# One tile of a windowed-attention and SwiGLU kernel written in token order, its last rows projected as 384 and 128 columns

## The chip, the cores and the metric

The kernel runs on one core of a Trainium2 chip. The metric is device time in microseconds: the median of repeated runs. A profile of one execution shows where that time goes. Engines are named as the profile names them: PE is the matrix engine (PEld its weight load), DVE the vector engine, ACT the scalar engine, POOL GpSimd, and SP the engine that only issues transfers and waits.

## The reference

The reference is attention in a sliding window, followed by a gated feed-forward block on the joined heads:

```python
# q, k, v: (8, 8, 576, 64)
scores = np.matmul(q, k.transpose(0, 1, 3, 2)) / np.sqrt(64)
mask = (rel >= 0) & (rel < 64)          # rel = query position - key position
attn = softmax of the masked scores
x = np.matmul(attn, v), heads joined: (4608, 512)
g = x @ w_gate                          # 512 -> 1536
out = (g * sigmoid(g)) * (x @ w_val) @ w_out   # -> (4608, 512) float32
```

## The kernel before

The 4608 tokens are nine tiles of 512 (`NT = 9`). Tiles 0 to 6 are the first 512 tokens of batches 0 to 6; tile 7 (`LAST`) gathers the 64 remaining tokens of each of the eight batches; tile 8, the last in order, is the first 512 tokens of batch 7. All engines' programs are written out by hand in the order of the code; nothing is reordered by a planner.

For one tile the work is this. `turn_q` and `turn_k` (DVE) transpose the staged queries and keys, which POOL loaded with `load_qk`. `scores` multiplies keys with queries, ACT takes the exponential, DVE masks it. `sums` multiplies the weights with ones (`totals`, line 294), and ACT turns those sums into inverses by a logarithm (`log`, line 304) and an exponential (`invert`, line 307). `mix_all` multiplies the values with the weights (line 347), and `scale` (line 359) multiplies each of the four results, 128 x 512 in PSUM, with the inverse sums, giving `xT`. `gate_value` then runs 12 blocks of four matmuls for the gate and four for the value (line 401); ACT applies SiLU (394) and DVE multiplies into `hT` (395). `project` multiplies 128 columns of `hT` at a time with `w_out` (12 matmuls, line 410), copies the 128 x 512 result to SBUF (`project_end`, line 417) and stores it.

The 512 tokens of a tile do not stand in order. For tile 0 (`t < TURNED`, `TURNED = 1`) column 128 e + x of `xT` is token 4 x + e, for the others column 32 e + x is token 16 x + e. The 128 rows that come out of one `project` are therefore four runs of 32 rows, and the rows of one run lie 16 rows apart in the output. So a tile other than tile 0 needs four stores of 32 rows each per `project`:

```python
for i in range(4):
    eng = nc.scalar if t == NT - 1 and i % 2 else nc.sync
    eng.dma_start(rows[4 * s + i], os_[32 * i:32 * i + 32])
```

In tile 0 one store takes all 128 rows (line 420). In tile 8, where nothing follows, every second store is issued by ACT in place of SP.

The attention of tile t is interleaved with the projection of tile t-1; the gate blocks of tile t carry the turns of tile t+1. Tile 8's projection stands alone at the end: `project` for the row groups 0, 1 and 2, then `project_last` for group 3. That one works in two halves of 256 columns (24 matmuls, line 446), copies each half as it is done (line 450) and stores it in four pieces (line 453), so eight stores in all.

A transfer from SP or ACT reports its landing on one of eight semaphores. At the end of the program SP waits for these in turn (line 717), and then all engines meet before the program ends.

The functions that the change touches follow, with the line numbers that the profile uses.

Of the kernel before, what the change touches and what calls it, by code (L numbers as in the profile page):

```python
# [8 lines left out]
P = 128  # L9
# [8 lines left out]
def kernel(  # L18
# [10 lines left out]
    nc = tc.nc  # L29
    S, D, H = 576, 64, 8  # L30
    NTOK, DFF, DM = 4608, 1536, 512
    NT = NTOK // 512
    TURNED = 1
# [15 lines left out]
    wo = cst.tile([P, 12, DM], BF16, name="wo")  # L49
# [12 lines left out]
    def batch(t):  # L62
        return t if t < LAST else t - 1
# [7 lines left out]
    staged, queries, weights, inverse, xT, hT = {}, {}, {}, {}, {}, {}  # L71
# [169 lines left out]
    def half(x):  # L241
        return slice(64 * x, 64 * x + 64)
# [48 lines left out]
    def totals(t, w, d):  # L291
        for h in range(2):
            for x in range(2):
                nc.tensor.matmul(  # L294
                    d[x][half(h)].rearrange("r (e j y) -> r j e y", e=16, j=8),
                    ones[half(x), 0:D],
                    weights[t, w, h][1][half(x)].rearrange("r j (e y) -> r j e y", e=16),
                )

    def room(n):  # L300
        return fsb.tile([P, 2, 512], FP32, name="r", tag="r", bufs=4)[:, 0:n]

    def log(r, d_ps):
        nc.scalar.activation(r, d_ps, AF.Ln)  # L304

    def invert(r):
        nc.scalar.activation(r, r, AF.Exp, scale=-1.0)  # L307

    def sums(t, w):
        d = d_tile(), d_tile()  # L310
        totals(t, w, d)
        for x in range(2):
            r = room(1)[:, 0]
            log(r, d[x])
            invert(r)
            inverse[t, 2 * w + x] = r

    def sums_wide(t, w):
        d_ps, r = wide("d_ps"), room(2)
        totals(t, w, (d_ps[:, 0], d_ps[:, 1]))  # L320
        for x in range(2):
            inverse[t, 2 * w + x] = r[:, x]
        log(r, d_ps[:])
        invert(r)
# [31 lines left out]
    def scale(t, u, o_ps):  # L356
        if u == 0:
            xT[t] = att.tile([P, 4, 512], BF16, name="xT", tag="xT")
        nc.vector.tensor_mul(xT[t][:, u, :], o_ps, inverse.pop((t, u)))  # L359

    def values_first(u, o_ps):
        mix_first(u, o_ps)
        scale(0, u, o_ps)

    def wide(name):
        return ps_a.tile([P, 2, 512], FP32, name=name, tag="a")

    def d_tile():
        return ps_f.tile([P, 512], FP32, name="d_ps", tag="v")[:]

    def mix_all(t):
        tiles = wide("ao_ps"), wide("ao_ps")
        for w in range(2):
            mix(t, w, (tiles[w][:, 0], tiles[w][:, 1]))
        for u in range(4):
            scale(t, u, tiles[u // 2][:, u % 2])
# [38 lines left out]
    def project_end(t, s, o_ps, copy=nc.vector.tensor_copy):  # L415
        os_ = fsb.tile([P, 512], FP32, name="os_", tag="os_", bufs=4)
        copy(os_[:], o_ps[:])
        rows = out[S * batch(t):S * batch(t) + 512]
        if t < TURNED:
            nc.sync.dma_start(rows.rearrange("(r e) f -> e r f", e=4)[s], os_[:])  # L420
            return
        if t == LAST:
            rows = out.rearrange("(b s) f -> b s f", s=S)[:, 512:S]
            rows = rows.rearrange("b (r e) f -> e b r f", e=16)
        else:
            rows = rows.rearrange("(r e) f -> e r f", e=16)
        for i in range(4):
            eng = nc.scalar if t == NT - 1 and i % 2 else nc.sync
            eng.dma_start(rows[4 * s + i], os_[32 * i:32 * i + 32])

    def out_tile():
        return ps_f.tile([P, 512], FP32, name="o_ps", tag="g")

    def project(t, s):
        o_ps = out_tile()
        project_part(t, (s,), (o_ps,), range(12))
        project_end(t, s, o_ps)

    def project_last(t, s):
        rows = out[S * batch(t):S * batch(t) + 512].rearrange("(r e) f -> e r f", e=16)  # L440
        os_ = fsb.tile([P, 512], FP32, name="os_", tag="os_", bufs=4)
        tiles = out_tile(), out_tile()
        for x in range(2):
            f = slice(256 * x, 256 * x + 256)
            for c in range(12):
                nc.tensor.matmul(  # L446
                    tiles[x][:, 0:256], hT[t][:, c, P * s:P * s + P], wo[:, c, f],
                    start=(c == 0), stop=(c == 11),
                )
            nc.vector.tensor_copy(os_[:, f], tiles[x][:, 0:256])  # L450
            for i in range(4):
                eng = nc.scalar if i % 2 else nc.sync
                eng.dma_start(rows[4 * s + i][:, f], os_[32 * i:32 * i + 32, f])

    def set_exp():
        nc.scalar.preload_act_table_set("natural_log_exp_and_others")  # L456
# [27 lines left out]
    for a in range(2):  # L484
        tr = tri[64 * a:64 * a + 64]
        nc.gpsimd.affine_select(
            out=tr[:, 1 - a], in_=tr[:, 1 - a], compare_op=ALU.is_ge, fill=0.0,
# [3 lines left out]
            out=tr[:, a], in_=tr[:, a], compare_op=ALU.is_ge, fill=0.0,  # L491
# [78 lines left out]
    d_ps, r = wide("d_ps"), room(2)  # L570
    for u in range(2):
        totals_first(u, d_ps[:, u])
        inverse[0, u] = r[:, u]
    log(r, d_ps[:])
    invert(r)
    scores_first(3)
# [27 lines left out]
    for m in range(12):  # L604
# [15 lines left out]
        if 5 <= m < 9:  # L620
            u = m - 5
            join(on_a, keys[:, u], raw_k[:, 2 * u:2 * u + 2])
        if 6 <= m < 10:
            u = m - 6
# [8 lines left out]
    tiles = [ps_f.tile([P, 512], FP32, name="o_ps", tag=x) for x in "gvgv"]  # L633
# [15 lines left out]
    for s in range(4):  # L649
        project_end(0, s, tiles[s], on_a if s < 2 else on_v)  # L650

    for t in range(1, NT):
        if t > 1:
            set_exp()
            scores(t, 0)
            project(t - 1, 0)
            if t == 2:
                stage_v(3)
            o_ps = out_tile()
            project_part(t - 1, (1,), (o_ps,), range(5))  # L660
            scores(t, 1)
            sums(t, 0)
            project_part(t - 1, (1,), (o_ps,), range(5, 12))
            project_end(t - 1, 1, o_ps)
            project(t - 1, 2)
            sums(t, 1)
            mix_all(t)
            project(t - 1, 3)
# [21 lines left out]
    for s in range(3):  # L690
        project(NT - 1, s)
    project_last(NT - 1, 3)

# [28 lines left out]
```

## Time and profile before

| | |
|---|---|
| median of 3 runs | 328.39 us (328.15 to 329.25) |
| span of the profiled execution, first to last instruction | 326.2 us |
| PE busy | 315.9 us, 97% of the span |
| DVE busy | 220.2 us, 67% |
| ACT busy | 167.2 us, 51% |
| POOL busy | 142.8 us, 44% |
| granted PE clock, mean | 0.999 |

The profile gives no other time for the profiled execution than its span. The median of the runs is 2.2 us longer; that part lies outside of the first and the last recorded instruction. In the profile's rows an instruction group is given by line, engine, operation, what it writes and reads, its shape and count; then the busy time and the mean of one in ns, and the idle time before it with what ended it. In the chain of work that ended last, each piece is the one that released the next. In a timeline, rows marked SPq or ACTq are transfers being issued: the time is that of the issuing, not of the data.

### The profile page before, as it was taken

The numbers are of one execution on the slowest core, as the hardware profiler recorded it, in microseconds if no ns is written. First come the engines' busy times: TensorE is split into PE (matmuls) and PEld (weight loads), VectorE is DVE, ScalarE is ACT, GpSimd is POOL, SyncE is SP. The second block draws the span as 40 slices with busy tenths as digits, with TensorE's granted clock in tenths as the row PEclk, the third lists the DMA queues.
The fourth block names the chain that finished last, engine by engine and source line by source line (L and its number), as shares of the span: only waits on it lengthen the run. The fifth ranks groups of instructions, "written<-read, shape, count | busy, mean of one in ns | idle before, by whom it ended". The sixth has DMA issues, their size and how long they took to land.

```text
span 326.2 us, 6959 instructions
## 1 busy us (share of the span) xinstructions
PE 315.9 (97%) x2700; PEld 150.7 (46%) x2743; DVE 220.2 (67%) x352; ACT 167.2 (51%) x239; POOL 142.8 (44%) x256
## 2 busy tenths in 40 slices
PE   8899999999999999999999999999999999999995
PEld 3444444444444444444444544454444544444443
DVE  5865755587766776887678766876697586773431
ACT  5855557337733683358336743565347633773300
POOL 5944545986085893586024989464200000000000
PEclk9999999999999999999999999999999999999999
DMA  7999999999789999959812999799401300020013
GB/s 253 200 202 202 206 146 215 170 146 143 164 160 206 138 151 205 192 81 214 175 38 29 169 173 92 53 191 195 97 2 34 99 0 2 16 83 32 2 33 98
DMA packets 82865, 40.84 MB, mean 125 GB/s; under 512 B 64272, under 2 KB 78352, under 8 KB 82832
## 3 DMA queue, kind: packets, MB, share of 16 engines
q0 software_dynamic: 50672, 23.08, 57.7%
q1 hardware_dynamic: 31136, 16.26, 19.3%
q10 hardware_dynamic: 1024, 1.05, 1.1%
q8 instruction: 21, 0.34, 0.4%
q14 instruction: 12, 0.10, 0.1%
HBM read 54.00 MB, written 9.44 MB: 194 GB/s over the span
## 4 chain that ended last, share of the span: by engine, by line
PE 86%; DMA 8%; POOL 3%; issue 1%; DVE 1%; SPq 0%; DVEq 0%; POOLq 0%
PE o_ps L410 28%; PE g_ps L401 26%; PE v_ps L401 25%; DMA wv<-in_moe_w_val_dram 4%; DMA q_s<-in_q_dram 3%; PE s_ps L261 3%; PE ao_ps L347 2%; PE d_ps L294 1%; DMA q_f<-in_q_dram 1%; POOL wg L172 1%; POOL wv L172 1%; PE o_ps L446 1%; POOL v L129 1%; POOL qk_b L517 0%; DVE qT L198 0%
## 5 line engine op out<-in xcount | busy, mean ns | idle before, releaser
L394 ACT ACTIVATE sg<-g_ps 128x512 f32<-128x512 f32 x108 | 64.4, 597 | 113.8 <-PE g_ps L401 85.1
L395 DVE TENSOR_TENSOR hT<-sg,v_ps 128x512 bf16<-128x512 f32 x108 | 74.7, 693 | 59.8 <-PE v_ps L401 49.2
L401 PE MATMUL g_ps<-xT,wg 128*128 128x512 bf16 x415 | 108.2, 379 | 0.9
L401 PE MATMUL v_ps<-xT,wv 128*128 128x512 bf16 x415 | 107.2, 379 | 0.1
L410 PE MATMUL o_ps<-wo,hT 128*128 128x512 bf16 x396 | 93.6, 380 | 1.5 <-issue 0.3
L108 POOL DMA_DIRECT2D k_s<-in_k_dram x112 | 60.6, 552 | 26.2 <-DMA q_s<-in_q_dram 15.3
L401 PEld LDWEIGHTS <-wv 128*128 128x128 bf16 x424 | 41.5, 98 | 50.1
L401 PEld LDWEIGHTS <-wg 128*128 128x128 bf16 x424 | 41.3, 98 | 49.5 <-issue 0.6
L410 PEld LDWEIGHTS <-hT 128*128 128x128 bf16 x420 | 39.1, 98 | 46.5 <-issue 1.8
L274 ACT ACTIVATE eb<-s_ps 128x960 bf16<-128x960 f32 (+1 forms) x32 | 29.5, 974 | 16.4 <-PE s_ps L261 16.3
L208 DVE STREAM_TRANSPOSE kT<-k_s 128x512 bf16<-128x512 bf16 x28 | 36.0, 1284 | 0.3 <-issue 0.3
L277 DVE TENSOR_TENSOR eb<-eb,mask 128x960 bf16<-128x960 bf16 (+1 forms) x32 | 21.1, 658 | 14.4 <-ACT eb L274 14.4
L359 DVE TENSOR_TENSOR xT<-ao_ps,r 128x512 bf16<-128x512 f32 x36 | 23.0, 684 | 6.5 <-PE ao_ps L347 4.8
L162 POOL CAST vb<-v_f 128x512 bf16<-128x512 f32 x20 | 11.4, 618 | 31.9 <-DMA v_f<-in_v_dram 22.1
L304 ACT ACTIVATE r<-d_ps 128x512 f32<-128x512 f32 (+1 forms) x33 | 20.8, 629 | 6.2 <-PE d_ps L294 5.9
L198 DVE STREAM_TRANSPOSE qT<-q_s 128x512 bf16<-128x512 bf16 x32 | 22.4, 702 | 0.8 <-DMA q_s<-in_q_dram 0.8
L307 ACT ACTIVATE r<-r 128x512 f32<-128x512 f32 (+1 forms) x33 | 22.0, 669 | 1.0
L88 POOL DMA_DIRECT2D q_s<-in_q_dram x28 | 15.2, 564 | 10.2 <-DVE qT L198 4.8
L137 POOL DMA_DIRECT2D vb<-in_v_dram x16 | 10.9, 710 | 8.7 <-DMA wo<-in_moe_w_out_dram 3.7
L282 DVE TENSOR_TENSOR both<-eb 128x512 bf16<-128x512 bf16 x32 | 13.6, 425 | 1.1
L456 ACT ACT_TABLE_LOAD x9 | 11.5, 1283 | 2.0 <-issue 1.9
L95 POOL DMA_DIRECT2D q_s<-in_q_dram x16 | 8.6, 629 | 7.4 <-DVE qT L198 7.4
(107 smaller groups left out, 185.2 us busy)
## 6 DMA issues: line engine op xcount, KB each, us to landing
q_s<-in_q_dram POOLq DMA_DIRECT2D x28, 248.0 KB, 6.0
k_s<-in_k_dram POOLq DMA_DIRECT2D x112, 56.0 KB, 4.8
v_f<-in_v_dram SPq DMA_DIRECT2D x40, 128.0 KB
wo<-in_moe_w_out_dram POOLq DMA_DIRECT2D x3, 512.0 KB, 12.3
q_f<-in_q_dram SPq DMA_DIRECT2D x4, 256.0 KB
vb<-in_v_dram POOLq DMA_DIRECT2D x16, 64.0 KB, 2.9
v<-in_v_dram POOLq DMA_DIRECT2D x16, 64.0 KB, 3.1
q_s<-in_q_dram POOLq DMA_DIRECT2D x16, 62.0 KB, 3.6
```

The source lines that it names most:

```text
L108: nc.gpsimd.dma_start(k_s[p0:p0 + 32, g, :, 0:w], k[b, a:H:2, s:s + P].rearrange("u (r e) d -> r u (e d)", e=4) [:, :, 32 * c:32 * c + w],)
L198: nc.vector.transpose(queries[t][:, u, :].rearrange("r (e x) -> r e x", e=16), staged[t][0][:, u].rearrange("r (e d) -> r e d", d=D)[:, :, ...
L208: nc.vector.transpose(dst[:, u, :].rearrange("r (g x e) -> r g e x", g=4, e=4), k_s[:, :, u].rearrange("r g (e d) -> r g e d", d=D)[:, :, ...
L274: nc.scalar.activation(flat, s_ps[h][:].rearrange("r a b -> r (a b)")[:, 0:n], AF.Exp, scale=0.125)
L277: nc.vector.tensor_mul(flat, flat, mask[:].rearrange("r j c e y -> r (j c e y)")[:, 0:n])
L304: nc.scalar.activation(r, d_ps, AF.Ln)
L307: nc.scalar.activation(r, r, AF.Exp, scale=-1.0)
L359: nc.vector.tensor_mul(xT[t][:, u, :], o_ps, inverse.pop((t, u)))
L394: nc.scalar.activation(sg[:], g_ps[:], AF.Silu)
L395: nc.vector.tensor_mul(hT[t][:, m, :], sg[:], v_ps[:])
L401: nc.tensor.matmul(ps[:], w[:, c, P * m:P * m + P], xT[t][:, c, :], start=(c == 0), stop=(c == 3),)
L410: nc.tensor.matmul(o_ps[:], hT[t][:, c, P * s:P * s + P], wo[:, c, :], start=(c == 0), stop=(c == 11),)
```

## The change

The diff, with all that changes the program:

```diff
+    def turned(ap):
+        return ap.rearrange("r (e x) -> r x e", e=16)
+
     def sums(t, w):
...
             r = room(1)[:, 0]
-            log(r, d[x])
+            if t == NT - 1:
+                log(r.rearrange("r (x e) -> r x e", e=16), turned(d[x]))
+            else:
+                log(r, d[x])
             invert(r)
             inverse[t, 2 * w + x] = r
...
     def scale(t, u, o_ps):
         if u == 0:
             xT[t] = att.tile([P, 4, 512], BF16, name="xT", tag="xT")
-        nc.vector.tensor_mul(xT[t][:, u, :], o_ps, inverse.pop((t, u)))
+        x, r = xT[t][:, u, :], inverse.pop((t, u))
+        if t == NT - 1:
+            x, o_ps = x.rearrange("r (x e) -> r x e", e=16), turned(o_ps)
+            r = r.rearrange("r (x e) -> r x e", e=16)
+        nc.vector.tensor_mul(x, o_ps, r)
...
         copy(os_[:], o_ps[:])
         rows = out[S * batch(t):S * batch(t) + 512]
-        if t < TURNED:
-            nc.sync.dma_start(rows.rearrange("(r e) f -> e r f", e=4)[s], os_[:])
+        if t < TURNED or t == NT - 1:
+            if t < TURNED:
+                rows = rows.rearrange("(r e) f -> e r f", e=4)[s]
+            else:
+                rows = rows[P * s:P * s + P]
+            if t < TURNED or s == 0:
+                for i in range(2):
+                    nc.sync.dma_start(rows[half(i)], os_[half(i)])
+            else:
+                nc.sync.dma_start(rows, os_[:])
             return
...
         for i in range(4):
-            eng = nc.scalar if t == NT - 1 and i % 2 else nc.sync
-            eng.dma_start(rows[4 * s + i], os_[32 * i:32 * i + 32])
+            nc.sync.dma_start(rows[4 * s + i], os_[32 * i:32 * i + 32])
...
     def project_last(t, s):
-        rows = out[S * batch(t):S * batch(t) + 512].rearrange("(r e) f -> e r f", e=16)
+        r0 = S * batch(t) + P * s
         os_ = fsb.tile([P, 512], FP32, name="os_", tag="os_", bufs=4)
-        tiles = out_tile(), out_tile()
-        for x in range(2):
-            f = slice(256 * x, 256 * x + 256)
+        for f0, f1 in ((0, 384), (384, 512)):
+            o_ps = out_tile()
             for c in range(12):
                 nc.tensor.matmul(
-                    tiles[x][:, 0:256], hT[t][:, c, P * s:P * s + P], wo[:, c, f],
+                    o_ps[:, 0:f1 - f0], hT[t][:, c, P * s:P * s + P], wo[:, c, f0:f1],
                     start=(c == 0), stop=(c == 11),
                 )
-            nc.vector.tensor_copy(os_[:, f], tiles[x][:, 0:256])
-            for i in range(4):
-                eng = nc.scalar if i % 2 else nc.sync
-                eng.dma_start(rows[4 * s + i][:, f], os_[32 * i:32 * i + 32, f])
+            nc.vector.tensor_copy(os_[:, f0:f1], o_ps[:, 0:f1 - f0])
+            nc.sync.dma_start(out[r0:r0 + P, f0:f1], os_[:, f0:f1])
```

In tile 8 alone, `sums` and `scale` read their PSUM operand with a step of 32 elements, so that the inverse sums and `xT` stand in token order. ACT's logarithm does the reordering for the sums, DVE's multiplication for the values; no instruction is added in either. From `xT` on, tile 8's tokens are in order, and the 128 rows of a `project` are 128 rows of the output, one behind the other.

The stores of tile 8 are then these, all issued by SP: row group 0 in two halves of 64 rows, groups 1 and 2 in one store of 128 rows each, and group 3 as one store of 384 columns and one of 128 columns. Before there were 20: 12 for groups 0 to 2 and eight for group 3. `project_last` splits its columns 384 and 128 in place of 256 and 256.

There is one more thing in the diff: in tile 0 the store of 128 rows becomes two halves of 64 rows, four times, so SP issues eight stores there in place of four. Its other operations stay as they were.

## The prediction

> **What bounds the kernel now.** I read the page's chain first: PE alone carries 86% of it. A change that leaves PE's instructions alone can only move the time where PE waits, or where the chain has left PE: behind the last matmul.
>
> ```profile
> PE 86%; DMA 8%; POOL 3%; issue 1%; DVE 1%; SPq 0%; DVEq 0%; POOLq 0%
> ```
>
> So I took the timeline of the end, the waits of SP, and the DMA share of the last 6.3 us (40 slices of 0.158 us from 320.0).
>
> ```profile
> 319.51 2.78 PE L446 MATMUL o_ps<-wo,hT 128*128 128x256 bf16 x24
> ...
> 321.02 0.42 DVE L450 COPY os__4457<-o_ps 128x256 f32<-128x256 f32 x1 [0.62 <-PE o_ps L446]
> 321.47 2.09 SPq L453 DMA_DIRECT2D out_dram<-os__4457  x4
> 321.48 2.16 ACTq L453 DMA_DIRECT2D out_dram<-os__4457  x4
> 322.33 0.42 DVE L450 COPY os__4457<-o_ps 128x256 f32<-128x256 f32 x1 [0.89 <-PE o_ps L446]
> ```
> ```profile
> SPq L717 <- DMA out_dram<-os__4457: 1.2, 1, 1.2
> ```
> ```profile
> DMA  0000000287989968537500176276000000000000
> ```
>
> PE ends at 322.31. A copy of 0.42, then two stores one behind the other on each queue: SP's at 322.78 and 323.14, ACT's at 322.79 and 323.20. The last bytes move at 324.4 (last digit of the row), the last store reports at 324.87, 1.67 after its issue. SP, which had waited 1.2 us, passes its remaining semaphore waits, some 0.062 apart, until 325.39, and 0.84 later the program has ended (326.23). From PE's end to the span's end: 3.92 us. This stretch is what the change works on.
>
> The other place is the attention of tile 8, where ACT and DVE get the strided reads:
>
> ```profile
> 288.19 2.68 DVE L359 TENSOR_TENSOR xT<-ao_ps,r 128x512 bf16<-128x512 f32 x4 [0.16 <-PE ao_ps L347]
> ...
> 288.42 2.77 PE L410 MATMUL o_ps<-wo,hT 128*128 128x512 bf16 x11
> 288.90 0.58 ACT L304 ACTIVATE r<-d_ps 128x512 f32<-128x512 f32 x1
> ...
> 290.16 1.28 ACT L459 ACT_TABLE_LOAD   x1
> ...
> 291.02 1.03 PE L401 MATMUL g_ps<-xT,wg 128*128 128x512 bf16 x4
> ```
>
> Here twelve projection matmuls of tile 7 hide the scaling: DVE is done at 290.87, and the gate reads the fourth quarter of `xT` with its fourth matmul, at about 291.67. So 0.80 us are spare.
>
> **Part 1, PE in the last row group: 0.** 24 matmuls of 256 columns start 0.109 apart (2.63 us in the chain). The transposes of line 186 are 128 x 128 with a weight load each and start 0.055 apart, so a weight load (98 ns busy) does not hold back 128 columns; 512 columns run at 0.216. For 384 I take 0.163 between. 12 x 0.163 + 12 x 0.055 = 2.61. PE ends where it did.
>
> **Part 2, the last copy: -0.13.** 512 columns cost 0.69, 256 cost 0.42, so 128 columns cost 0.42 - 0.13 = 0.29. It starts at 322.33 as now and ends at 322.62. The copy of 384 columns, 0.42 + 0.13 = 0.56, starts near 321.67, ends at 322.22, and is out of the way.
>
> **Part 3, the last stores: -0.5.** SP issues the 384-column store at 322.25. Whole 128-row stores took this to issue in tile 0:
>
> ```profile
> L420 SPq DMA_DIRECT2D out_dram<-os__895 x1: 360/360/360, 53.2 to 53.2; - x1
> ...
> L420 SPq DMA_DIRECT2D out_dram<-os__901 x1: 1275/1275/1275, 54.2 to 54.2; - x1
> ```
>
> With 0.36 (three of the four took 0.35 to 0.40, the 1.275 stood in a saturated DMA), a look at the next semaphore and the gap, the second store goes out at 322.73, 0.47 before the last one now. How long does it take to land? A store of 32 descriptors of 1 KB begins to move 0.85 after its issue; a load of 512 descriptors (tile 8's values, issued at 225.43, little else moving) began 1.3 after and then moved all 512 in 0.6. So 128 descriptors should begin after 0.9 to 0.95. The 384-column store moves from 323.2 on; its eight packets of 1.5 KB per DMA engine take some 65 ns each, by tile 0's whole stores (84 to 96 ns per 2 KB): until 323.7. The second is queued behind it on the same engines, eight packets of 512 B, 0.2 in all, and reports 0.35 after its last byte as now: 324.25, against 324.87. That is 1.5 after its issue; the part from the copy's end (0.13) is in it. Bounds: 324.1 if the first store does not hold it up, 325.0 if 128 descriptors need 2.3, a share between 32 descriptors (1.6) and the first loads of the kernel (256 descriptors, 3.3), which would be 0.15 worse than now. I take 324.25, nearer to the 512-descriptor load, since that one ran alone and the first loads shared the engines with seven others: -0.62 for parts 2 and 3 together.
>
> **Part 4, SP's closing waits: -0.43.** The eight landing semaphores rotate with each transfer, and the closing waits take them in a fixed order. Now the last store stands on the first of the eight, so 0.5 us of waits follow it. Between the first store of tile 0 and the end the change issues four stores more in tile 0 and fourteen fewer in tile 8 (6 for 20); counting through, the last store falls on the last of the eight, and one wait of 0.06 follows. If the order is another than before, up to 0.43 of this is lost. ACT's stores in the tail go away, and nothing waits for ACT.
>
> **Part 5, the first three stores of the tail: 0.** Now at 315.25, 317.84 and 320.43, four each on two queues; then on SP two halves, one, one. DVE's copies are 2.6 apart and each store is issued in under 1 us; the last of them has moved before 322.3.
>
> **Part 6, strided reads: 0, bounds 0 and +1.1.** No row shows a PSUM read of f32 with a step. The nearest is `split_k`, which reads bf16 from PSUM with a step of 256 B, in the groups of instructions (busy us, then mean ns of one):
>
> ```profile
> L189 DVE COPY kT<-tp 128x512 bf16<-128x512 bf16 x8 | 5.5, 682 | 0.6 <-PE tp L186 0.6
> ...
> L531 DVE COPY qT<-tp 128x512 bf16<-128x512 bf16 x3 | 1.3, 417 | 0.8 <-PE tp L186 0.8
> ```
>
> With the step it takes 682, as long as f32 without one (680 to 692, line 417), not twice that; only the quick contiguous bf16 copy is lost. The four multiplications are f32 already (686): I take no change. For ACT's logarithm there is no such row. If it doubled (590 to 1.1 us), the fourth inverse would come 1.15 late, the last `scale` with it, and PE would wait 1.15 - 0.80 = 0.4. If DVE doubled as well, the four multiplications would take 4.9 from 288.2 and overrun by 1.1. A gain is excluded: no step is taken out. The Trainium skill's page "Advanced Engine Details and Errata", section PSUM Cachelines, speaks against the change: PSUM has lines of 8 bytes, and two consecutive elements should lie together for best throughput; a step of 128 B never does that. The row of line 189 does not show this penalty for DVE; by the rule the sum would be nearer to +0.1 than to -1.
>
> **Part 7, tile 0's half stores: 0, bounds 0 and +0.7.** SP has no other work between 56 and 79 us, so the four added issues (0.36 to 0.40) are hidden. But the DMA engines are at 9 tenths from 53 to 62, and tile 2's keys, still being loaded, are turned at 63.71, where DVE had waited 0.27. DVE then multiplies block 5 one us late; PE does not notice because its second pair of PSUM tiles covers some 0.75. The bytes are the same. If half stores moved at the 130 ns per 2 KB of 32-row stores on a quiet chip rather than 87, the engines would be busy 512 x 43 ns / 16 = 1.4 longer, and PE would lose 1.4 - 0.75 = 0.65. In loaded stretches (222 to 225 us) 32-row stores took 92 to 96 ns, so I take 0. The Trainium skill ("DMA: Bandwidth & Descriptors", Rules for kernel authors) advises against the halves: two transfers of disjoint partition halves share the same engines and serialize, so one of 128 partitions should be used. No row shows what that costs here, and a price it does not give.
>
> **Sum.** -0.62 - 0.43 = -1.05 on the span of 326.23, so 325.2; with the 2.2 us that lie around it, 327.3 against the median of 328.39.
>
> **The rivals.** *A, as summed: 0.60.* 326.9 (-1.2 and 0.3 of scatter) to 327.8 (no gain in the closing waits). Its threshold of 0.3%, 1.0 us, which is about what a measurement of this kernel can tell from no change, cuts through this case: 0.42 beyond it, 0.18 within.
> *B, the single store lands late: 0.17.* 128 descriptors need 1.9 to 2.3 us from issue: landing at 324.6 to 325.0, and little is gained but the order of the waits: 327.7 to 328.1, within. For it: two queues share the issuing now, and the first loads took long. Against it: 512 descriptors moved in 0.6.
> *C, strided reads cost: 0.13.* ACT doubled 327.7, both doubled 328.4; within, and 0.02 beyond it on the slow side for a higher price.
> *D, tile 0's halves delay tile 2: 0.10, slower.* The place is the turn at 63.71; each us by which the keys come later than 0.75 is lost on PE. From 1.8 late on it is slower than before; if the halves doubled the 4.7 us that the stores' data took (55.0 to 59.7), with 4.7 more of queue, PE would lose up to 4 and end at 331; half of it gives 329.4. For it: the engines are full there and the third whole store was held for 1.275. Against it: the same bytes.
>
> Faster 0.42; same 0.18 + 0.17 + 0.11 = 0.46; slower 0.02 + 0.10 = 0.12. The range from 326.9 to 328.8 holds A, B and nearly all of C.
>
> **What would show it.** Right: line 446 still some 2.6 us; the last copy 0.29; two SP issues and none of ACT behind it; last data near 324.0, SP's last wait under 1.2, and about 2.85 from PE's end to the span's end. Line 304 at 590 and line 359 at 686 in the window of tile 8, `g_ps` still starting at 291.0. Wrong: either of those near 1.1 us; an idle PE between 62 and 70; a last store that lands 2 us after its issue.

## The result and the profile after

The changed kernel takes 327.41 us (median of 13 runs, 326.98 to 328.52) against 328.72 us for the kernel before in the same comparison: a ratio of 0.9965, with a 95% interval of 0.9953 to 0.9977. It is faster by 0.35%, between 0.8 and 1.5 us. Two more comparisons of the same two kernels, made with the experiments, gave 0.9976 (0.9967 to 0.9986) and 0.9968 (0.9949 to 0.9986). As times the three are 1.15, 0.79 and 1.05 us, 1.0 on average. The profiled execution took 327.56 us, with a span of 325.6 us (326.2 before).

The page's chain after the change, by engine, with PE at 87% in place of 86:

```profile
PE 87%; DMA 8%; POOL 3%; DVE 1%; issue 0%; SPq 0%; DVEq 0%; POOLq 0%
```

The timeline of the end (start us, us, engine, line, what; SPq rows are the issuing of transfers). `project_last`'s matmuls are now line 463, its copies line 467, its stores line 468:

```profile
319.82 2.78 PE L463 MATMUL o_ps<-wo,hT 128*128 128x384 bf16 x24
320.02 0.69 DVE L428 COPY os__4450<-o_ps 128x512 f32<-128x512 f32 x1 [1.90 <-DMA out_dram<-os__4434]
320.74 0.36 SPq L439 DMA_DIRECT2D out_dram<-os__4450  x1
321.97 0.96 DVE L467 COPY os__4453<-o_ps 128x384 f32<-128x384 f32 x2 [1.26 <-PE o_ps L463]
322.55 0.81 SPq L468 DMA_DIRECT2D out_dram<-os__4453  x2
```

PE needs as long for its 24 matmuls as before (2.78). The two copies are one merged row here: 0.56 from 321.97, then 0.29 from 322.64. Two issues of SP follow, and none of ACT. SP's own waits show what is left of the 1.2 us for the last landing:

```profile
SPq L732 <- DMA out_dram<-os__4453: 0.7, 1, 0.7
```

The DMA share in 40 slices of 0.158 us, here from 319.4 us: one block for each store of the row groups 1 and 2, and the last two stores as a single block that ends at 324.28.

```profile
DMA  9800000000000089994000000599994000000000
```

The two engines with strided reads, in the window of tile 8 (median in the middle of the three ns):

```profile
L308 ACT ACTIVATE r<-d_ps x4: 578/589/604, 284.9 to 289.2; 128x512 f32<-128x512 f32 x4
```
```profile
L370 DVE TENSOR_TENSOR xT<-ao_ps,r x4: 678/686/692, 288.5 to 290.5; 128x512 bf16<-128x512 f32 x4
```

The span shrank by 0.67 us, but the tail by more: its first matmul stands at 319.82, 0.31 later than before (0.12 of it by tile 0's first scaling, 0.17 between tile 1 and tile 2). So I measure each profile from that matmul on. In the table "landing" is from there to the last report of a store, "closing" from there to the span's end; both come from the trace's records of the semaphores. "Keys" is how long after tile 1's first scaling DVE turned tile 2's first keys, "interval" the time from tile 1's first scaling to tile 2's.

| kernel | ratio to before (95%) | landing | closing | sum | keys | interval |
|---|---|---|---|---|---|---|
| before | | 5.36 | 1.36 | 6.72 | 12.63 | 33.22 |
| changed | 0.9965 (0.9953 to 0.9977) | 4.82 | 0.92 | 5.74 | 13.39 | 33.39 |
| changed, 2nd | 0.9976 (0.9967 to 0.9986) | 4.80 | 0.92 | 5.72 | 12.80 | 33.22 |
| changed, 3rd | 0.9968 (0.9949 to 0.9986) | 4.80 | 0.92 | 5.72 | 13.30 | 33.31 |
| tile 0 whole | 0.9981 (0.9973 to 0.9990) | 4.85 | 1.16 | 6.00 | 12.29 | 33.22 |
| rotation, by tile 0 | 1.0001 (0.9990 to 1.0011) | 5.43 | 0.98 | 6.41 | 13.67 | 33.67 |
| rotation, by tile 5 | 0.9983 (0.9971 to 0.9995) | 5.43 | 0.98 | 6.40 | 12.29 | 33.22 |
| strided reads alone | 0.9996 (0.9987 to 1.0005) | 5.42 | 1.36 | 6.78 | 12.29 | 33.22 |
| 256 and 256 | 0.9978 (0.9969 to 0.9987) | 4.96 | 0.92 | 5.88 | 13.05 | 33.22 |
| 256, 128, 128 | 0.9968 (0.9955 to 0.9980) | 4.71 | 0.91 | 5.62 | 12.91 | 33.22 |
| last stores halved | 1.0036 (1.0024 to 1.0049) | 6.44 | 1.28 | 7.72 | 13.05 | 33.22 |
| halved, even and odd | 1.0028 (1.0014 to 1.0043) | 6.41 | 1.28 | 7.70 | 12.29 | 33.22 |
| six tiles in order | 0.9980 (0.9970 to 0.9990) | 4.82 | 1.14 | 5.95 | 12.60 | 33.22 |
| all together | 0.9959 (0.9946 to 0.9972) | 4.70 | 0.92 | 5.62 | 12.44 | 33.22 |

The later intervals, from tile 2 on, agree to 0.02 us in all fourteen profiles. What differs ahead of the tail is the start: tile 0's first scaling stands at 14.5 to 15.7 us, and tile 1's follows after 36.3 to 37.1, so that it stands at 50.9 to 52.2. That scatter is as large as the gain, and it is why a single span says little here while the tail says much.

### The profile page after: what moved, and what is told of

Read it like the earlier page. It is cut to its first block, busy times and chain, and to the rows that moved or that the text cites. A ratio compares the mean times of both kernels' runs of the same rounds, so it can differ in the third digit from the quotient of the medians.

```text
span 325.6 us, 6987 instructions
## 1 busy us (share of the span) xinstructions
PE 318.5 (98%) x2743; PEld 150.6 (46%) x2743; DVE 219.7 (68%) x352; ACT 167.2 (51%) x239; POOL 143.0 (44%) x256
## 4 chain that ended last, share of the span: by engine, by line
PE 87%; DMA 8%; POOL 3%; DVE 1%; issue 0%; SPq 0%; DVEq 0%; POOLq 0%
PE o_ps L421 29%; PE g_ps L412 26%; PE v_ps L412 26%; DMA wv<-in_moe_w_val_dram 4%; DMA q_s<-in_q_dram 3%; PE s_ps L261 3%; PE ao_ps L354 2%; PE d_ps L294 1%; DMA q_f<-in_q_dram 1%; POOL wg L172 1%; POOL wv L172 1%; PE o_ps L463 1%; POOL v L129 1%; POOL qk_b L532 0%; DVE qT L198 0%
## 5 line engine op out<-in xcount | busy, mean ns | idle before, releaser
L412 PE MATMUL v_ps<-xT,wv 128*128 128x512 bf16 x424 | 108.8, 379 | 0.0
L421 PE MATMUL o_ps<-wo,hT 128*128 128x512 bf16 x420 | 95.2, 380 | 0.0
L162 POOL CAST vb<-v_f 128x512 bf16<-128x512 f32 x20 | 11.5, 621 | 29.7 <-DMA v_f<-in_v_dram 17.9
L88 POOL DMA_DIRECT2D q_s<-in_q_dram x28 | 15.2, 557 | 10.3 <-DVE qT L198 4.2
L471 ACT ACT_TABLE_LOAD x9 | 11.5, 1283 | 2.0 <-issue 1.9
L474 ACT ACT_TABLE_LOAD x9 | 11.5, 1283 | 0.2
## 6 DMA issues: line engine op xcount, KB each, us to landing
wo<-in_moe_w_out_dram POOLq DMA_DIRECT2D x3, 512.0 KB, 12.3
```

The source lines that it names most:

```text
L412: nc.tensor.matmul(ps[:], w[:, c, P * m:P * m + P], xT[t][:, c, :], start=(c == 0), stop=(c == 3),)
L421: nc.tensor.matmul(o_ps[:], hT[t][:, c, P * s:P * s + P], wo[:, c, :], start=(c == 0), stop=(c == 11),)
```

## The experiments

**The changed kernel again**, as the mark for others.

> The changed kernel once more, as the mark for the others of this call. From the first matmul of the last row group to the span's end 5.73 us (6.72 before), of which 4.81 to the last landing and 0.92 behind it. Both theories of the gain (the tail alone; the tail and something earlier) expect 0.3 to 0.4% below the kernel before; if the part of the span ahead of the last row group is again 0.3 longer than before, something earlier costs, if it is equal or shorter it was scatter.

> The changed kernel, as the mark for the others of this call: 5.73 us from the last row group's first matmul to the end; tile 2's first keys turned 12.8 to 13.4 us after tile 1's first scaling (12.3 to 12.6 with whole stores in tile 0). If that comes under 13.2, tile 1 to tile 2 takes 33.22 us, and each us over 13.2 is added to it.

Landing and closing came out within 0.02 us each time. The part ahead of the tail was longer in one (320.44) and nearly equal in the other (319.69), so most of it is scatter of the start. A small share is not: the keys, below.

**Tile 0's stores whole again.**

```diff
-            if t < TURNED or s == 0:
+            if t == NT - 1 and s == 0:
                 for i in range(2):
```

> The changed kernel with tile 0's four stores whole again, so four stores fewer. If the closing waits go by the rotation of the eight semaphores, the last store now stands on the fourth of them: behind its landing 0.92 + 4 x 0.062 = 1.17 us, and 5.98 from the last row group's first matmul, time about 0.25 above the changed kernel. Rival: tile 0's half stores delay the keys of tile 2; then PE ahead of the last row group is 0.3 or more shorter here, and the time equal or lower.

Closing took 1.16 (1.17 expected). The last store now reported on the fourth of the eight semaphores, and the four waits behind it cost 0.24. In time the two kernels can't be told apart (0.9981 and 0.9976 in the same comparison). The four half stores in tile 0 thus do nothing for tile 0. They place the last store in the rotation. The rival has its sign too: the keys come at 12.29 here. But nothing is gained by that as long as they come before 13.2.

**Rotation alone, by tile 0 and by tile 5.** The kernel before with six stores more, once in tile 0 (ten in place of four), once in tile 5 (six of the 32-row stores as two of 16):

```diff
-            nc.sync.dma_start(rows.rearrange("(r e) f -> e r f", e=4)[s], os_[:])
+            rows = rows.rearrange("(r e) f -> e r f", e=4)[s]
+            cuts = (0, 32, 64, 128) if s < 2 else (0, 64, 128)
+            for a, b in zip(cuts, cuts[1:]):
+                nc.sync.dma_start(rows[a:b], os_[a:b])
```
```diff
-            eng.dma_start(rows[4 * s + i], os_[32 * i:32 * i + 32])
+            if t == 5 and s < 3 and i < 2:
+                for a in (0, 16):
+                    eng.dma_start(rows[4 * s + i][a:a + 16], os_[32 * i + a:32 * i + a + 16])
+            else:
+                eng.dma_start(rows[4 * s + i], os_[32 * i:32 * i + 32])
```

> The kernel before with tile 0's stores cut into ten in place of four, and nothing else: six places in the rotation, so that the last two stores stand on the last two of the eight semaphores. If the closing waits are on the path, 0.92 to 0.98 us behind the last landing in place of 1.36, landing itself unchanged at 5.36 after the last row group's first matmul; time 0.4 lower. Rival: SP's waits run beside something as long; then 1.36 again and no gain.

> The kernel before with six stores of tile 5 cut in two, tile 0 untouched: the same rotation by six places as in the run where tile 0 had ten stores, but where nothing is waiting. If that run lost its gain to the late keys, this one has keys at 12.3 to 12.6, 33.22 from tile 1 to tile 2, 0.98 behind the last landing, and is 0.3 to 0.4 faster than the kernel before. Rival: the closing waits do not count in the measured time; then the time is that of the kernel before although the span's end is nearer.

Both tails came out alike, 0.98 behind the landing and 6.4 in all, but only the second kernel was faster: 0.9983 (0.9971 to 0.9995). In the first the gain was spent in tile 1. Its DVE timeline there shows the wait for the keys:

```profile
64.81 1.32 DVE L208 STREAM_TRANSPOSE kT<-k_s 128x512 bf16<-128x512 bf16 x1 [1.31 <-DMA k_s<-in_k_dram]
65.95 1.29 DVE L395 TENSOR_TENSOR hT<-sg,v_ps 128x512 bf16<-128x512 f32 x2
```

In the kernel before, the same turn starts a microsecond earlier, after a wait of 0.27:

```profile
63.71 1.32 DVE L208 STREAM_TRANSPOSE kT<-k_s 128x512 bf16<-128x512 bf16 x1 [0.27 <-issue]
64.84 1.44 DVE L395 TENSOR_TENSOR hT<-sg,v_ps 128x512 bf16<-128x512 f32 x2
```

There the chain stays with PE:

```profile
64.62 0.86 PE v_ps L401 x4
65.48 0.86 PE g_ps L401 x4
66.35 0.86 PE v_ps L401 x4
```

With ten stores in tile 0 it leaves PE in the same stretch:

```profile
64.67 0.88 PE v_ps L401 x4
65.55 0.03 issue
65.58 0.02 DVEq L395
65.60 0.35 issue
65.95 0.71 DVE hT L395
66.66 0.04 issue
66.70 1.02 PE v_ps L401 x4
```

The turn stands in DVE's program ahead of the multiplication that frees a PSUM tile for PE. The keys came late, the turn with them, the multiplication behind it ended at 66.66, and PE resumed at 66.70. The interval grew by 0.45, which is more than the 0.31 that the tail gained. This is the prediction's rival D, with its place and its mechanism. The second kernel, whose rotation is the same and whose keys are in time (12.29), keeps its gain: so the closing waits do count in the measured time.

**The strided reads alone.** The kernel before, with `sums` and `scale` of tile 8 as changed, and the 20 stores as before, to the rows that now hold these tokens:

```diff
+                log(r.rearrange("r (x e) -> r x e", e=16), turned(d[x]))
...
+            x, o_ps = x.rearrange("r (x e) -> r x e", e=16), turned(o_ps)
...
+            rows = rows.rearrange("(e r) f -> e r f", e=16)
```

> The kernel before with tile 8 in token order by the strided reads, its 20 stores of 32 rows and 256 and 256 columns as before, only to other rows of the output. If strided reads cost nothing: logarithm 590 ns, multiplication 686 ns, 6.72 us from the last row group's first matmul to the end, time as before. Rivals: reads at a step of 128 B cost elsewhere (time above before by 0.3 or more), or stores to adjacent rows land faster by themselves (last landing under 5.2 after that first matmul).

The logarithm took 590 ns and the multiplication 685:

```profile
L307 ACT ACTIVATE r<-d_ps x4: 579/590/606, 284.5 to 288.8; 128x512 f32<-128x512 f32 x4
```
```profile
L369 DVE TENSOR_TENSOR xT<-ao_ps,r x4: 679/685/692, 288.1 to 290.1; 128x512 bf16<-128x512 f32 x4
```

The time is the old one, 0.9996 (0.9987 to 1.0005), and the landing is the old one too (5.42). Token order is free, and stores to adjacent rows of the output are not faster for that. What token order buys is that one store can take 128 rows.

**256 and 256 columns.**

```diff
-        for f0, f1 in ((0, 384), (384, 512)):
+        for f0, f1 in ((0, 256), (256, 512)):
```

> The changed kernel with 256 and 256 columns in place of 384 and 128. By the sum the last copy ends 0.13 later and twice the bytes move behind it: last landing 5.0 after the last row group's first matmul (4.81 with 384 and 128), end 0.2 later. Rival: the data of the first store is what holds the second; then half of it less ahead of the last store gives 4.8 or below.

```profile
321.60 1.64 SPq L468 DMA_DIRECT2D out_dram<-os__4453  x2
322.45 0.42 DVE L467 COPY os__4453<-o_ps 128x256 f32<-128x256 f32 x1 [0.88 <-PE o_ps L463]
```

Landing 4.96 against 4.81: the split is worth 0.15, and the step from 20 stores on two queues to whole stores on one is worth the rest, 5.36 - 4.96 = 0.40 (the four profiles with the old tail land at 5.36 to 5.43). That rest is issuing: the last store goes out 3.27 after the first matmul, against 3.69 in the kernel before, and lands as long after its issue, 1.69 against 1.67. The rival, that the first store's data hold the second, would by itself have made the landing shorter. The packet records show what outweighs it: the second store's data begin 0.83 after the issue in place of 0.92, but 128 KB then take 0.52 where 64 KB take 0.38, and the longer copy puts the issue 0.11 later. The times (0.9978 and 0.9976 in the same comparison) can't tell the two splits apart; the records can.

**Three pieces.**

```diff
-        for f0, f1 in ((0, 384), (384, 512)):
+        for f0, f1 in ((0, 256), (256, 384), (384, 512)):
...
-            if t < TURNED or s == 0:
+            if t < TURNED:
```

> The changed kernel with the last row group in 256, 128 and 128 columns, and row group 0 stored whole, so that the count of stores, and with it the order of the closing waits, stays. If the last store waits behind the 192 KB of the one before it, it now lands 1.45 to 1.5 after its issue in place of 1.66: 4.6 from the last row group's first matmul, 5.5 to the span's end, time 0.2 below the changed kernel. Rival: issue and receipt are fixed; then 4.8 and 5.7 again, or worse by what a third copy and issue put in the way.

```profile
321.85 1.54 SPq L468 DMA_DIRECT2D out_dram<-os__4452  x3
322.06 0.29 DVE L467 COPY os__4452<-o_ps 128x128 f32<-128x128 f32 x1 [0.24 <-PE o_ps L463]
322.74 0.29 DVE L467 COPY os__4452<-o_ps 128x128 f32<-128x128 f32 x1 [0.39 <-PE o_ps L463]
```

The last store landed 1.53 after its issue in place of 1.65, and its data began 0.83 after the issue in place of 0.92, so some of that time was indeed the wait behind 192 KB. Landing 4.71: half of the expected gain, because 36 matmuls take PE 0.04 longer than 24 and the landing was expected after 1.45 to 1.5. In time it is 0.9968 where the changed kernel beside it had 0.9976: not told apart.

**The last stores in halves of 64 rows**, once the lower and the upper rows, once the even and the odd:

```diff
-            nc.sync.dma_start(out[r0:r0 + P, f0:f1], os_[:, f0:f1])
+            for i in range(2):
+                nc.sync.dma_start(out[r0:r0 + P, f0:f1][half(i)], os_[half(i), f0:f1])
```
```diff
+            for i in range(2):
+                nc.sync.dma_start(out[r0 + i:r0 + P:2, f0:f1], os_[i:P:2, f0:f1])
```

> The changed kernel with each of the last two stores cut into two of 64 rows. If whole stores of 128 rows are what shortens the landing, each half takes about 0.55 to issue and its packets 145 ns per 2 KB in place of 86: the last landing 0.6 later, 5.4 after the last row group's first matmul. The rotation moves by two, so the last store stands on the second of the eight: 0.92 + 6 x 0.062 = 1.3 behind the landing, 6.7 in all, no gain left against the kernel before. Rival: the same bytes on the same sixteen DMA engines land at the same time, 4.8 to 4.9.

> The changed kernel with each of the last two stores cut into even and odd rows of 64. If 64 adjacent rows are slow because they lie in one half of the partitions, every second row is as fast as all of them: packets near 86 ns per 2 KB, the last landing 5.4 after the last row group's first matmul (four issues of 0.55 in a row remain). Rival: it is the count of 64 that is slow; then 6.4 again, as with the two halves.

Both were slower than the kernel before, and the landing came 1.6 later, not 0.6. The issues, of the halves, then of the even and odd rows, then of the changed kernel's two whole stores (ns min, median, max):

```profile
L469 SPq DMA_DIRECT2D out_dram<-os__4453 x4: 472/568/592, 323.0 to 324.8; - x4
```
```profile
L469 SPq DMA_DIRECT2D out_dram<-os__4453 x4: 503/567/588, 323.3 to 325.1; - x4
```
```profile
L468 SPq DMA_DIRECT2D out_dram<-os__4453 x2: 332/358/383, 322.6 to 323.0; - x2
```

Four issues in a row put the last one at 4.54 to 4.57 after the first matmul (3.16 with two), and it then took 1.84 to 1.90 to land, not 1.65. The DMA shares show the other half of the question. Halves, from 322.5 in slices of 0.128, then even and odd rows, from 322.5 in slices of 0.133:

```profile
DMA  9500000000003998228982162001620000000000
```
```profile
DMA  9988100000000029810395004400053000000000
```

The blocks of the even and odd rows are shorter: their packets of 1.5 KB took some 65 ns, as in whole stores, those of 64 adjacent rows some 100. So the expectation for the data held and the one for the end failed. What sets the end is the issuing, and that is slow for 64 rows whichever they are. The Trainium skill ("SBUF — State Buffer", Door 1: The DMA port swizzle) says that 64 adjacent partitions reach half of the 16 ports that a DMA uses; the packet times agree, but no run here counts ports. Its advice against halves ("DMA: Bandwidth & Descriptors", Rules for kernel authors) gives as the reason that both halves share the same engines. Halves did cost 1.6 us here, but most of it is the issuing (the last store goes out 1.4 later).

**Six tiles in token order**, tile 0 whole.

```diff
+    def in_order(t):
+        return t > 1 and t != LAST
...
-            if t == NT - 1:
+            if in_order(t):
...
-        if t == NT - 1:
+        if in_order(t):
...
-        if t < TURNED or t == NT - 1:
+        if t < TURNED or in_order(t):
...
-            if t < TURNED or s == 0:
+            if t == NT - 1 and s == 0:
```

> Tiles 2 to 6 and 8 all in token order, each with one store of 128 rows per row group, and tile 0's stores whole; 64 stores fewer, so the rotation ends where it does in the changed kernel. Theory: the strided reads stay at 590 and 686 ns in all six tiles and the stores of tiles 2 to 6 are hidden by PE, so the tail is 5.73 and the time that of the changed kernel within 0.3. Rivals: fewer and better stores free the DMA engines for the loads, and PE ahead of the tail gets 0.3 or more shorter; or the reads cost where DVE is fuller, and it gets longer.

```profile
L373 DVE TENSOR_TENSOR xT<-ao_ps,r 128x512 bf16<-128x512 f32 x36 | 23.0, 685 | 6.4 <-PE ao_ps L357 4.8 <-PE ao_ps L340 0.6 <-ACT r L311 0.4
L311 ACT ACTIVATE r<-d_ps 128x512 f32<-128x512 f32 x30 | 17.7, 590 | 4.7 <-PE d_ps L294 4.7
```

The reads cost nothing in six tiles either, and 60 stores fewer in tiles 2 to 6 gave nothing: the intervals are those of the kernel before to 0.02. PE hides it all. The closing was 0.22 longer than expected in this profile because DVE came late to the last meeting of the engines, behind SP's waits; the next kernel, which has the same in it, took 0.92.

**All together.** The last kernel, with whole stores for every row group and three pieces at the end:

```diff
-            if t == NT - 1 and s == 0:
-                for i in range(2):
-                    nc.sync.dma_start(rows[half(i)], os_[half(i)])
-            else:
-                nc.sync.dma_start(rows, os_[:])
+            nc.sync.dma_start(rows, os_[:])
...
-        for f0, f1 in ((0, 384), (384, 512)):
+        for f0, f1 in ((0, 256), (256, 384), (384, 512)):
```

> All that paid, together: tiles 2 to 6 and 8 in token order, whole stores everywhere, the last row group in 256, 128 and 128 columns, and the count of stores such that the last one stands on the last of the eight semaphores. 5.6 us from the last row group's first matmul to the end, first keys turned at 12.3 to 12.6 and 33.22 from tile 1 to tile 2 every time. Time 1.1 below the kernel before, 0.1 to 0.2 below the changed one. Rival: what whole stores in tiles 2 to 6 do to the DMA is felt elsewhere; then an interval between tiles differs from 33.22 or 33.89.

```profile
321.35 1.55 SPq L467 DMA_DIRECT2D out_dram<-os__4388  x3
321.57 0.29 DVE L466 COPY os__4388<-o_ps 128x128 f32<-128x128 f32 x1 [0.24 <-PE o_ps L462]
322.24 0.29 DVE L466 COPY os__4388<-o_ps 128x128 f32<-128x128 f32 x1 [0.38 <-PE o_ps L462]
```

327.06 us, a ratio of 0.9959 (0.9946 to 0.9972), with the shortest tail (5.62, as with three pieces alone) and keys in time. It is the fastest kernel here by its median, but against the changed one (0.9968 in the same comparison) the intervals overlap.

## Why the prediction was right, step by step

The forecast was 327.3 us, by 1.05 less in the tail; the tail came out 0.98 shorter (6.72 to 5.74), the time at 327.41. The sum was right for its own reasons, and most terms can be checked one by one. That the two times agree to 0.1 us is in part luck: the forecast started from 328.39 (3 runs), and the kernel before took 328.72 beside the changed one (13 runs). The tail is the better check.

- *Part 1, PE: right.* The last matmul starts 2.56 after the first (2.51 before), and the last copy 2.82 after it in both.
- *Parts 2 and 3, -0.62: -0.54 measured.* The copy took the 0.29 that was worked out. The second store was issued 3.16 after the first matmul, where the working had 3.22. What was too small is the term from issue to landing: 1.65, not 1.5, and 1.67 in the kernel before, so that all of the 0.54 is the earlier issue (3.16 against 3.69). The data of the two stores moved without a gap until 324.28, and 0.35 later the store reported, as predicted; the first store's data began sooner, 0.83 after the issue and not 0.95, but lasted 0.69, not 0.5.
- *Part 4, closing waits, -0.43: -0.44 measured.* This came from counting the transfers modulo eight. Kernels that change the rotation confirm it: 1.28 with six semaphores behind the last store, 1.16 with four, 0.98 with one.
- *Part 5, first three stores: right.* The two halves of 64 rows took 0.54 and 0.58 to issue, longer than the stores before (0.31 to 0.43) but under the 1 us that the working allowed. They were hidden: row group 2's copy starts 0.20 after the first matmul, as before.
- *Part 6, strided reads: 0, right*, and the row of line 189 was the right neighbour, for ACT as well. The rule on lines of 8 bytes in PSUM ("Advanced Engine Details and Errata", PSUM Cachelines), by which the sum would have been near +0.1, does not show in these reads.
- *Part 7, tile 0's halves: taken as 0; measured 0 to 0.17.* With halves the keys came at 12.8 to 13.4 in six of seven profiles (12.3 to 12.6 with whole stores), and the last data of tile 0's stores moved until 11.5 to 12.1 after the scaling (9.0 to 9.5). Up to 13.05 nothing is lost, and nothing was measured between 13.05 and 13.30; 13.30 cost 0.09, 13.39 cost 0.17, 13.67 (ten stores) cost 0.45, each of them what it is beyond 13.22. The mechanism of rival D was right and its slack of 0.75, from 12.63, was 0.59. Its size, up to 4 us, was far too high. In the trace's records the last of these key loads landed 3.9 to 5.4 us after its issue in all seven profiles with halves, and 2.3 to 3.7 in the six with whole stores; in the seventh its issue stood early enough (7.0 after the scaling, 7.3 to 9.4 in the other six) for the keys to be in time. The working of the cover failed on one point: each issue was to take 0.36 to 0.40, and took 0.54 to 0.62 (one 1.18), and the stores' data ended some 2.5 later.
- *B* fell: 1.65 from issue to landing, against 1.9 to 2.3. Its figure is that of larger stores: the 128 rows of 384 columns took 1.92, those of 512 columns 2.04. *C* fell with the reads.

Left open: why the issue of 64 rows takes longer than that of 128. No run separated the count of rows from what else the issue has to do. Nor did a run issue the last two whole stores from two queues.

## What to carry to other kernels

Where PE carries the chain, a change that leaves PE's work alone gains only where the chain leaves PE. Behind its last instruction three things count: how late the last transfer is issued, how many issues and bytes stand ahead of it on its queue, and how many waits remain behind its landing. The last is a matter of counting transfers: here a store more or less, in tile 0 or in tile 5, moved it by 0.06 us a step, 0.44 in all. When the change is of the size of the scatter of the spans, measure each profile from an event behind which everything is repeatable, and look at the intervals between such events for the rest.

## What was not expected of the hardware

- In the tail a store of 64 rows took 0.47 to 0.59 us to issue, one of 128 rows 0.33 to 0.38, one of 32 rows 0.31 to 0.44 (with the DMA engines full, earlier in the program, single ones of each took over 1.1). Two halves cost about three times the issue of the whole.
- A step of 128 bytes costs ACT and DVE nothing when they read f32 from PSUM: 589 and 686 ns, as without.
- 64 every-second rows move at the packet time of a whole store (65 ns per 1.5 KB), 64 adjacent ones at about 100.
